# Beacon attention feeding a two-layer MLP: the first q and k loads move from the hardware queues to the software queue, and the planner's orders around them change

## The chip, the cores and the metric

The kernel runs on one core of a Trainium2 chip. The metric is the device time of one execution in microseconds (us), smaller is better. The time before is the median of 10 runs. All times below are from runs of the kernel before, or from one execution of it taken with the hardware profiler.

## The reference, cut to what matters

```
k_all = concat([beacon_k, k], axis=2)        # 16 beacons + 576 keys, per batch (8) and head (8), D = 64
v_all = concat([beacon_v, v], axis=2)
scores = (q @ k_all^T) / 8                   # causal over the 576, beacons always seen
a = exp(scores - max) / (sum + 1e-9)
x = (a @ v_all) as [8*576 tokens, 512]
h = x @ w_in                                 # 512 -> 2048
out = (h * sigmoid(1.702 h)) @ w_out         # 2048 -> 512, float32
```

Inputs are float32 in HBM; the kernel computes in float16 with float32 sums in PSUM.

## The kernel before, in words

The attention is cut into 32 *pairs*: pair i is batch i // 4 and two heads. For each pair the scores are made keys by queries, in four chunks of columns: `qk_chunk` on PE (TensorE) into one of two score tiles `s`, then `exp_chunk` on ACT into one of two tiles `E`, then the causal part is masked by `mask_chunk`, on DVE or POOL. Then the sums against `vb` follow on PE: for pairs 0 to 3 `av_both`, whose part z = 1 multiplies the ones columns of `vb` (the sums of the softmax) and whose part z = 0 multiplies the values; later pairs use `av_half`. DVE turns the sums into reciprocals and writes the normalised rows to `xT` (`norm_both`, `norm`). When 512 tokens of `xT` are there, `mlp1` (64 matmuls, L516) and its activation (`mlp1_gelu`, L528) run, and its four `mlp2` blocks (L538) are laid between the pairs that follow. The first `mlp1` needs the rows of pairs 0 to 3.

q and k must stand with D on the partitions. For batches 0 and 1 PE transposes them (`tr_pe`, L190) out of the tile `g`, and `tr_pe_out` (L198) copies the result from PSUM to `qT` and `kT`; a transpose of k or q serves one pair. For batches 2 to 7 DVE transposes squares (`tr_squares`, L253), DVE or POOL orders them (`tr_order`, L262), and SP writes them to DRAM and reads them back. Beacons of k of batches 0 and 1 come by `load_bk6` and `cast_bk6`; those of the other six by `load_bk` (8 DMAs on SP, L128) and one `cast_bk` (L136).

Two kinds of queues load. SP and ACT issue hardware-queue DMAs[...]. POOL issues the software queue, which converts float32 to float16 under way; it carries nearly all of q, k, v and the weights, in the order of POOL's instructions. POOL goes through a ring of eight semaphores: a DMA waits until the one eight places earlier has landed, and whatever stands behind it on POOL (masks, too) waits with it.

In the kernel before, q and k of the first two heads come as float32 on the hardware queues (`load_f32`: k on SP, q on ACT) into tiles `O`, and ACT and DVE cast them into `g` (`cast_f32`, L165).

The order on each engine is written by a planner in the kernel (`issue`): every piece of work is a `Work` with an engine or a choice of engines, a guessed duration, a key, needs, and "after" (not planned before that one's start). The planner only fixes the order of each engine's instructions; at run time an instruction waits for its data and its buffers, and for nothing else. Small fillers (`warm`, L1043, a matmul on zeros) are planned where PE would idle in the first 60 us. From the first `mlp1` on, the order on PE is mostly written out by `chain`.

Of the kernel before, what the change touches and what calls it, by code (L numbers as in the profile page):

```python
# [16 lines left out]
def kernel(  # L17
# [64 lines left out]
    def make_keep():  # L82
# [8 lines left out]
            channel_multiplier=-1,  # L91
        )

    w1t = cst.tile([P, NKP, DFF], F16, tag="w1", name="w1")
    w2t = cst.tile([P, NNT, DMODEL], F16, tag="w2", name="w2")
    xT = cst.tile([P, NKP, RING * S], F16, tag="xT", name="xT")
# [46 lines left out]
    def load_qk6(b, h0, h1, w):  # L143
        if b not in nat6:
            nat6[b] = gp.tile([TP, 2, H, TR * D], F16, tag="g", name="g")
        nc.gpsimd.dma_start(
            out=nat6[b][:, w, h0:h1, :],
            in_=(q, k)[w][b, h0:h1].rearrange("h (p t) d -> p h (t d)", t=TR),
        )

    def load_f32(w, eng):

        s = op_.tile([P, 2, S], F32, tag="O", name="O")
        stg[w] = s
        dict(SP=nc.sync, ACT=nc.scalar)[eng].dma_start(
            out=s.rearrange("p x s -> p (x s)")[0:TP, 0 : 2 * TR * D].rearrange(
                "p (h c) -> p h c", h=2
            ),
            in_=(q, k)[w][0, 0:2].rearrange("h (p t) d -> p h (t d)", t=TR),
        )  # L160

    def cast_f32(w, eng):
        if 0 not in nat6:
            nat6[0] = gp.tile([TP, 2, H, TR * D], F16, tag="g", name="g")
        copy[eng](  # L165
            out=nat6[0][:, w, 0:2, :].rearrange("p h c -> p (h c)"),
            in_=stg[w].rearrange("p x s -> p (x s)")[0:TP, 0 : 2 * TR * D],
        )

    def load_bk6(b):  # L170
# [148 lines left out]

    scs = {}  # L320

    def qk_chunk(i, ci):
        b, p = divmod(i, NPAIR)
        qT, kT = qTs[b % 2], kTs[b % 2]
        sc = pss.tile([P, 2, 512], F32, tag="s", name="s")
        scs[(i, ci)] = sc
        o = 0
        for (j, a, e) in CH[ci]:
            for x in range(2):
                r = 64 * x  # L330
                nc.tensor.matmul(  # L331
                    sc[:, x, o : o + e - a],
                    kT[r : r + 64, p, j * P : (j + 1) * P],
                    qT[r : r + 64, p, a:e],
                    start=True,
                    stop=True,
                )
            o += e - a

    def exp_chunk(i, ci):  # L340
# [240 lines left out]
    )  # L581
    SEM, QS = 0.1, 0.1
    SPL, CAP = 2.0, 2.0
    NBOTH = 4
    HWQ = 3

    def use(buf, *ws):
        buf.users += ws
# [2 lines left out]
    Lq, V, W1, W2 = {}, {}, [], []  # L591
    kTb, qTb, vbb, xTb = {}, {}, {}, {}
    placed = {}
    bkB = None
    pk = {}
    trp = {}
    mkeep = Work("POOL", 0.3, -4.95, make_keep)
    midn = Work("POOL", 0.6, -5.95, lambda: make_identity(nc, ident))

    bk6, stw, cst0 = {}, {}, {}  # L600
    stb = {w: Buf("O") for w in (1, 0, "bk")}
    stw[1] = Work("SP", 0.6, -9, lambda: load_f32(1, "SP"), alloc=stb[1], dma=0.7)
    stw[0] = Work("ACT", 0.6, -9, lambda: load_f32(0, "ACT"), alloc=stb[0], dma=0.7, after=[stw[1]])
    for b in range(NB2):
        ob = Buf("osb")
        x = Work("SP", 0.6, -8 + b, lambda b=b: load_bk6(b), alloc=ob, dma=0.1, after=[stw[1]])
        bk6[b] = Work(
            dict(ACT=0.6, DVE=0.6) if b else dict(ACT=0.6), 0, (-8, 1.5)[b],
            lambda eng, b=b: cast_bk6(b, eng), [x],
        )  # L610
        use(ob, bk6[b])
    g0 = Buf("g")
    for w in (1, 0):
        cst0[w] = Work(
            {("DVE", "ACT")[w]: 0.85}, 0, -8.5 - 0.1 * w, lambda eng, w=w: cast_f32(w, eng),
            [stw[w]],
        )
        use(stb[w], cst0[w])

    def first_loads(b):  # L620
        k0 = 4 * b
        kl = (-6, -4.4)[b]
        gb6 = g0 if b == 0 else Buf("g")
        lds = {(0, 1): cst0[1], (0, 0): cst0[0]} if b == 0 else {}
        got = []
        for (h0, h1) in ((2, 4), (4, H)) if b == 0 else ((0, 4), (4, H)):
            for w in (1, 0):
                x = Work(
                    "POOL", 0.7, kl + 0.1 * h0 + 0.02 * (1 - w) + (h0 == 4),
                    lambda b=b, h0=h0, h1=h1, w=w: load_qk6(b, h0, h1, w),  # L630
                    alloc=None if got else gb6, dma=0.37 * (h1 - h0), after=got[:1],
                )
                got.append(x)
                for p in range(h0 // 2, h1 // 2):
                    lds[(p, w)] = x
        if b == 0:
            for x in cst0.values():
                x.after.append(got[0])
        x = None
        for p in range(NPAIR):  # L640
            for w in (1, 0):
                if p == 1 and w == 1:
                    ub = Buf("u")
                    x = Work(
                        "PE", 0.3, k0, lambda b=b: tr_pe_beacon(b), [bk6[b], midn], alloc=ub,
                        after=[x],
                    )
                    y = Work(
                        dict(ACT=0.3, DVE=0.25), 0, k0, lambda eng, b=b: tr_pe_beacon_out(b, eng),
                        [x], after=[pk[(b, 0, 1)]],  # L650
                    )
                    use(ub, y)
                ub = Buf("u")
                kk = 4 * b + p - 0.5
                x = Work(
                    "PE", 0.55, kk, lambda b=b, p=p, w=w: tr_pe(b, p, w), [lds[(p, w)], midn],
                    alloc=ub, after=[x] if x else [],
                )
                use(gb6, x)
                trp[(b, p, w)] = x  # L660
                z = Work(
                    {("DVE", "ACT")[w]: 0.7} if b + p == 0 else dict(ACT=0.66, DVE=0.76), 0, kk,
                    lambda eng, b=b, p=p, w=w: tr_pe_out(b, p, w, eng),
                    [x], alloc=(qTb, kTb)[w][b] if p == 0 else None,
                    after=[pk[(b, 0, w)]] if p else (),
                )
                use(ub, z)
                pk[(b, p, w)] = z
        pk[b] = y
        if b == 0:  # L670
            bk6[1].after.append(pk[(0, 0, 1)])

    for b in range(B):
        kTb[b], qTb[b], vbb[b] = (Buf(f"{n}{b % 2}") for n in ("kT", "qT", "vb"))
# [4 lines left out]
        for g in range(2) if b >= NB2 else ():  # L679
            for w in (1, 0):  # L680
# [24 lines left out]
                need = []  # L705
                if w == 1:
                    if bkB is None:
                        ld4 = [
                            Work(
                                "SP", 1.2, -6 + x, lambda x=x: load_bk(x),  # L710
                                alloc=stb["bk"] if x == 0 else None, dma=0.2,
                            )
                            for x in range(HG)
                        ]
                        for x, y in zip(ld4, ld4[1:]):
                            y.after.append(x)
                        bkB = [Work(dict(ACT=0.85, DVE=0.85, POOL=0.9), 0, 3, cast_bk, ld4)]
                        use(stb["bk"], *bkB)
                    need = [Work(
                        "DVE", 0.25, k0, lambda b=b, g=g: tr_beacon(b, g),  # L720
                        bkB, after=cp[:1],
                    )]
# [45 lines left out]
    for i in range(NSTEP):  # L768
# [5 lines left out]
        for c in range(len(CH)):  # L774
            s_ = Buf("s")
            qk_ = Work(
                "PE", CHW[c] / 2400 + 0.05, i + (0, 0.01, 0.4, 0.41)[c],
                lambda i=i, c=c: qk_chunk(i, c),
                [pk[(b, p, 0)], pk[(b, p, 1)], pk[b]] if b < NB2
                else [placed[(b, hf, 0)], placed[(b, hf, 1)]],  # L780
                alloc=s_, mode=1,
            )
# [11 lines left out]
            exps.setdefault(i, []).append(ex)  # L794
            use(s_, ex)
            nm = sum(1 for (j, a, e) in CH[c] if a == s0s[j])
            mk = Work(
                dict(DVE=0.46 * nm, POOL=0.41 * nm), 0, i + 0.3,
                lambda eng, i=i, c=c: mask_chunk(i, c, eng), [ex, mkeep],
            )  # L800
            use(Eb, mk)
            for (j, a, e) in CH[c]:
                ready.setdefault(j, []).append(mk if a == s0s[j] else ex)
        vb_ = [V[(b, j)] for j in range(NJ)] + [on[b % 2]]
# [3 lines left out]
        if i < NBOTH:  # L808
            for z in (1, 0):
                for half in range(2):  # L810
# [1 line left out]
                    ub[(half, z)] = Buf("u")  # L812
                    js = sorted({j for (j, lo, hi, col) in mm})
                    av = Work(
                        "PE", sum(hi - lo for (j, lo, hi, col) in mm) / 2400 + 0.15,
                        i + 1.05 + 0.2 * (1 - z) + 0.1 * half,
                        lambda i=i, half=half, z=z: av_both(i, half, z),
                        [r for j in js for r in ready[j]] + vb_, alloc=ub[(half, z)],
                        after=avs[-1:],
                    )  # L820
                    avs.append(av)
# [65 lines left out]
        w.needs.append(exps[i][0])  # L887

    trp[(0, 1, 1)].after.append(qks[(0, 1)])
    bkB[0].after.append(exps[0][3])  # L890

# [70 lines left out]
    def issue():  # L964
# [7 lines left out]
        while todo:  # L972
            best = None
            for w in todo:
# [17 lines left out]
                        t = max([t] + [x.t1 + SEM + QS * w.mode for x in old.users])  # L992
                for a in w.after:
                    t = max(t, a.t0)
                eng = min(w.opts, key=lambda e: max(t, free[e]) + w.opts[e] + BIAS[t > 45].get(e, 0))
                t = max(t, free[eng])
                if w.dma:
                    t = max(t, landed[eng][-8] + CAP)
# [9 lines left out]
            if eng == "PE":  # L1008
                d += 0.1 * (w.mode != mode)
                mode = w.mode  # L1010
            if w.key >= 1e6 and t < 7:
                d = 0.43
            w.t0 = t
            free[eng] = t + d
# [63 lines left out]
```

The softmax here doesn't subtract the row's maximum and nothing guards it: scores larger than these inputs give would overflow.

## Time and profile before

| | |
|---|---|
| median of 10 runs | 368.17 us (367.43 to 368.67) |
| profiled execution, time | 368.0 us |
| its span, first to last instruction | 366.3 us |
| PE busy | 353.1 us, 96% of the span |
| DVE, ACT, POOL busy | 248.8, 228.2, 153.5 us |
| software queue | 49152 packets, 18.19 MB written, 49.2% of 16 engines' span |
| start of the first `mlp1` (L516) | 35.22 us |

Times inside the profile are counted from the start of the span; 1.7 us of the execution's time lie outside it. "Idle before" in brackets is the idle time of that engine just before, with what ended it. A DMA's "landing" is counted from the start of its issue.

### The profile page before, as it was taken

Reading aid. Unit: us, or ns where it says so; the run is one execution under the profiler, and the core shown is the slowest. Engines: PE = TensorE matmul, PEld = TensorE weight load, DVE = VectorE, ACT = ScalarE, POOL = GpSimd, SP = SyncE. Lnnn points to the kernel's source line nnn. Section 1 sums busy time; section 2 is a strip of 40 time slices with the busy share of each in tenths; the row PEclk is TensorE's granted clock in tenths of the full one; section 3 lists DMA queues with packets and bytes.
Section 4 is the critical chain, followed back from the end, with each engine's and each line's share of the span. In section 5 each row is a group of like instructions: output and inputs, shape, how many; then the busy total and the mean of one; then the engine's idle time right before and its main releaser. Section 6 shows DMA issues by size and latency. Waiting matters only on the chain.

```text
span 366.3 us, 6133 instructions
## 1 busy us (share of the span) xinstructions
PE 353.1 (96%) x2349; PEld 176.5 (48%) x2349; DVE 248.8 (68%) x421; ACT 228.2 (62%) x335; POOL 153.5 (42%) x264
## 2 busy tenths in 40 slices
PE   7788999999999999999999999999999999999995
PEld 3355444444444444544455864544444454444442
DVE  5556499999999986998599949972995183010021
ACT  4678787648765776676857675677658724616200
POOL 9668567593368245754376236611430010000000
PEclk9989999999999999999999999999999999999999
DMA  9999999995699645894479537921100011000012
GB/s 142 150 206 189 188 236 236 218 115 101 194 235 174 129 130 143 129 169 138 126 108 145 163 119 136 142 80 32 59 30 29 2 57 57 2 29 29 30 57 86
DMA packets 69788, 43.41 MB, mean 119 GB/s; under 512 B 42624, under 2 KB 62080, under 8 KB 69760
## 3 DMA queue, kind: packets, MB, share of 16 engines
q0 software_dynamic: 49152, 18.19, 49.2%
q1 hardware_dynamic: 20400, 24.55, 21.3%
q8 instruction: 18, 0.29, 0.3%
q10 hardware_dynamic: 208, 0.29, 0.3%
q14 instruction: 10, 0.08, 0.1%
HBM read 44.60 MB, written 16.61 MB: 167 GB/s over the span
## 4 chain that ended last, share of the span: by engine, by line
PE 83%; DMA 8%; DVE 3%; ACT 3%; issue 1%; POOL 0%; SPq 0%; DVEq 0%; ACTq 0%
PE u L516 34%; PE u L538 34%; PE u L401 9%; PE s L331 6%; DMA g<-in_k_dram 4%; ACT E L344 2%; DMA O<-in_beacon_k_dram 2%; DMA osb<-in_beacon_k_dram 1%; DVE xT L489 1%; DVE zt L470 1%; DVE osb L551 1%; DVE O L459 1%; ACT L344 0%; POOL E L367 0%; ACT bk L136 0%
## 5 line engine op out<-in xcount | busy, mean ns | idle before, releaser
L344 ACT ACTIVATE E<-s 128x1024 f16<-128x1024 f32 (+3 forms) x128 | 103.6, 865 | 49.6 <-PE s L331 47.7
L538 PE MATMUL u<-w,g 128*128 128x512 f16 x576 | 129.2, 380 | 0.6 <-DVE O L459 0.4
L516 PE MATMUL u<-xT,w 128*128 128x512 f16 (+1 forms) x640 | 126.0, 358 | 0.0
L528 ACT ACTIVATE g<-u 128x512 f16<-128x512 f32 x144 | 85.1, 597 | 42.7 <-PE u L516 42.4
L367 POOL TENSOR_SCALAR_AFFINE_SELECT E<-E 128x256 f16<-128x256 f16 (+2 forms) x148 | 64.5, 455 | 83.5 <-ACT E L344 83.3
L516 PEld LDWEIGHTS <-w 128*128 128x128 f16 x640 | 62.0, 98 | 61.4 <-issue 0.9
L538 PEld LDWEIGHTS <-g 128*128 128x128 f16 x576 | 54.5, 98 | 65.4 <-issue 3.6
L551 DVE COPY osb<-u 128x512 f32<-128x512 f32 x30 | 20.5, 683 | 65.3 <-PE u L538 65.0
L459 DVE COPY O<-u 128x240 f32<-128x240 f32 (+1 forms) x84 | 34.8, 440 | 24.7 <-PE u L401 22.4
L262 POOL COPY t<-sq 128x576 f16<-128x576 f16 x21 | 26.7, 1272 | 48.2 <-DVE sq L253 41.9
L401 PE MATMUL u<-E,vb 128*128 128x240 f16 x392 | 46.7, 266 | 0.2
L489 DVE TENSOR_TENSOR xT<-O,rz 64x576 f16<-64x576 f32 x56 | 44.3, 792 | 0.8
L470 DVE STREAM_TRANSPOSE zt<-O 64x576 f32<-64x576 f32 x56 | 43.1, 770 | 1.4
L401 PEld LDWEIGHTS <-vb 128*128 128x128 f16 x392 | 32.2, 98 | 17.2 <-issue 7.6
L331 PE MATMUL s<-qT,kT 64*128 64x80 f16 (+5 forms) x384 | 37.1, 287 | 2.9 <-ACT E L344 1.7
L253 DVE STREAM_TRANSPOSE sq<-n 128x576 f16<-128x576 f16 x48 | 34.8, 746 | 6.8 <-DMA n<-in_k_dram 6.4
L221 POOL DMA_DIRECT2D vb<-in_v_dram x40 | 34.4, 868 | 4.0 <-DMA w<-in_moe_w_in_dram 3.3
L262 DVE COPY t<-sq 128x576 f16<-128x576 f16 x27 | 26.9, 994 | 0.3
L331 PEld LDWEIGHTS <-kT 64*128 64x128 f16 x384 | 13.1, 95 | 27.1 <-issue 19.3
L480 DVE STREAM_TRANSPOSE rz<-rt 128x576 f32<-128x576 f32 x32 | 24.4, 763 | 0.6
L459 ACT COPY O<-u 128x336 f32<-128x336 f32 (+1 forms) x28 | 10.7, 429 | 2.9 <-PE u L401 2.7
L1043 PE MATMUL u<-wu 128*128 128x512 f16 x29 | 10.2, 448 | 1.3 <-DVE wu L1036 1.3
(44 smaller groups left out, 124.8 us busy)
## 6 DMA issues: line engine op xcount, KB each, us to landing
out_dram<-osb SPq DMA_DIRECT2D x36, 256.0 KB, 2.1
d<-t SPq DMA_DIRECT2D x12, 296.0 KB, 2.4
kT<-d SPq DMA_DIRECT2D x12, 296.0 KB, 3.5
n<-in_k_dram POOLq DMA_DIRECT2D x12, 288.0 KB, 5.0
n<-in_q_dram POOLq DMA_DIRECT2D x12, 288.0 KB, 6.2
d<-t SPq DMA_DIRECT2D x12, 288.0 KB, 2.4
qT<-d SPq DMA_DIRECT2D x12, 288.0 KB, 3.3
vb<-in_v_dram POOLq DMA_DIRECT2D x24, 128.0 KB, 5.6
```

Source lines behind the costliest of these rows:

```text
L253: nc.vector.transpose(sqs[(b, g, w)][:, c * n : (c + 1) * n, :, :], nat[(b, g, w)][:, c * n : (c + 1) * n, :],)
L262: copy[eng](out=tqk[(b, g, w)][:, e, o : o + S].rearrange("p (r t) -> p r t", t=TPP), in_=sqs[(b, g, w)][:, :, e, :].rearrange("p t r -> p ...
L331: nc.tensor.matmul(sc[:, x, o : o + e - a], kT[r : r + 64, p, j * P : (j + 1) * P], qT[r : r + 64, p, a:e], start=True, stop=True,)
L344: nc.scalar.activation(out=Es[i][:, :, choff[ci] : choff[ci] + w], in_=scs[(i, ci)][:, :, 0:w], func=AFT.Exp, scale=0.125,)
L367: nc.gpsimd.affine_select(out=blk, in_=blk, compare_op=ALU.is_ge, fill=0.0, base=mc, pattern=[[0, 2], [1, w]], channel_multiplier=-1,)
L401: nc.tensor.matmul(u[:, lo:hi], vb[0:kw, j, :, :].rearrange("r h c -> r (h c)")[:, o : o + 2 * D], E[0:kw, x, col : col + hi - lo], start= ...
L459: copy[eng](out=Os[i][:, x, AQ[half] : AQ[half + 1]], in_=avu[(i, x, half)][:, :])
L470: nc.vector.transpose(zst[i][0][64 * x : 64 * x + 64, :, :], Os[i][64 * (1 - x) : 64 * (1 - x) + 64, x, :])
L489: vec[eng].tensor_tensor(out=xT[r : r + 64, p, c : c + S], in0=Os[i][r : r + 64, x, :], in1=zst[i][2][r : r + 64, :], op=ALU.mult,)
L516: nc.tensor.matmul(u[:, o : o + w], w1t[:, kp, nt * P : (nt + 1) * P], xT[:, kp, m : m + w], start=(kp == 0), stop=(kp == NKP - 1),)
L528: nc.scalar.activation(out=gts[g][:, nt, :], in_=hu[(g, nt)][:, :], func=AFT.Gelu_apprx_sigmoid)
L538: nc.tensor.matmul(o[:, :], gts[g][:, nt, mt * P : (mt + 1) * P], w2t[:, nt, :], start=(nt == 0), stop=(nt == NNT - 1),)
```

## The change

- `load_f32`, `cast_f32` and the two casts are gone. q and k of heads 0 and 1 are now the first two DMAs of POOL's software queue, ahead of the making of `ident`; heads 2 and 3 follow behind `ident`, then `keep`, then the values of batch 0, then heads 4 and 5, and 6 and 7, in pieces of two heads where four were loaded at once.
- `load_bk` is planned after the first exp of pair 2 (`BKE = 2`), and `cast_bk` may go to any engine. On SP the order is now: the two `load_bk6`, then the eight DMAs of `load_bk`, then the rest.
- The part z = 1 of `av_both` no longer lists the values' loads among its needs; its guessed duration and some keys change. A tile `neg` is made by one DVE instruction; the masking on PE that would use it is switched off (`NMASK = 0`), so `pe_mask` is false everywhere and all masks stay as they are.
- The planner therefore gives other orders. On ACT the cast of the beacons (`cast_bk`) is gone from between the exps of pairs 0 and 1; it stands on POOL behind the mask of pair 4's first chunk. On PE the sums z = 1 of pair 0 stand ahead of the last two score chunks of pair 1, the values' part behind them. Before the exps of pair 2 ACT copies kT and qT of pair 2 and kT of pair 3; between those of pairs 2 and 3 it copies qT of pair 3 and kT, qT of pair 4; between those of pairs 3 and 4, kT of pair 5. `mlp1` now stands behind all of chunks 0 and 1 of pair 5 on PE, and the transposes of pairs 6 and 7 all stand behind `mlp1` (before, that of pair 6's k stood ahead of it and only chunk 0 of pair 5). On POOL the blocks j = 1 and j = 2 of batch 1's values are issued one behind the other, and all four masks of pair 3 that POOL makes (chunks 1 to 3) stand right behind them; before, the block j = 3 stood between the masks of chunk 1 and those of chunks 2 and 3.

From the second half of pair 4's sums on, the order on PE is the same in both.

```
-    mkeep = Work("POOL", 0.3, -4.95, make_keep)
-    midn = Work("POOL", 0.6, -5.95, lambda: make_identity(nc, ident))
-    stw[1] = Work("SP", 0.6, -9, lambda: load_f32(1, "SP"), alloc=stb[1], dma=0.7)
-    stw[0] = Work("ACT", 0.6, -9, lambda: load_f32(0, "ACT"), alloc=stb[0], dma=0.7, after=[stw[1]])
+    mkeep = Work("POOL", 0.3, -5.6, make_keep)
+    mneg = Work("DVE", 0.2, -5, make_neg, [mkeep])
+    midn = Work("POOL", 0.6, -5.97, lambda: make_identity(nc, ident))
...
-        for (h0, h1) in ((2, 4), (4, H)) if b == 0 else ((0, 4), (4, H)):
+        for (h0, h1) in ((0, 2), (2, 4), (4, 6), (6, H)) if b == 0 else ((0, 4), (4, H)):
             for w in (1, 0):
                 x = Work(
-                    "POOL", 0.7, kl + 0.1 * h0 + 0.02 * (1 - w) + (h0 == 4),
+                    "POOL", 0.7, kl + 0.1 * h0 + 0.02 * (1 - w) + (b == 0) * (h0 >= 4) + (b == 1) * (h0 == 4),
...
-                        "PE", sum(hi - lo for (j, lo, hi, col) in mm) / 2400 + 0.15,
+                        "PE", sum(hi - lo for (j, lo, hi, col) in mm) / 2400 + 0.06,
-                        [r for j in js for r in ready[j]] + vb_, alloc=ub[(half, z)],
+                        [r for j in js for r in ready[j]] + (vb_[-1:] if z else vb_), alloc=ub[(half, z)],
...
+                        sbk = Buf("O")
+                        bkl4 += [
...
-    bkB[0].after.append(exps[0][3])
+    bkl[1].after.append(exps[0][2])
+    bkl4[0].after.append(exps[BKE][0])
...
-            if w.key >= 1e6 and t < 7:
+            if w.key >= 1e6 and t < 5:
```

## The prediction

> **What bounds the kernel now.** I read the page first, then the chain that ended last, then the timelines of ACT and POOL over the first 36 us, then a table by windows. Page: PE is full from the third slice on; the DMA engines are full for the first nine slices (82 us).
>
> ```profile
> PE   7788999999999999999999999999999999999995
> DMA  9999999995699645894479537921100011000012
> ```
>
> So after about 65 us the time is PE's own work, and what a start-up change can win is an earlier first `mlp1`, handed on undiminished. The chain of waits, first 66 us:
>
> ```profile
> 6.50 8.09 DMA O<-in_beacon_k_dram
> ...
> 14.81 0.83 ACT bk L136
> ...
> 18.35 15.48 DMA g<-in_k_dram
> ...
> 33.87 0.45 PE u L190 x12
> 34.32 0.65 PE u L1043 x2
> 34.96 0.32 PE s L331 x2
> 35.28 13.93 PE u L516 x64
> 49.24 0.60 ACT g L528
> 49.85 1.28 ACT L344
> 51.15 3.14 ACT E L344 x4
> ```
>
> Two loads are on it: the beacons, for which ACT stops, and pair 6's k, which the transposes ahead of L516 wait for. But a chain shows one releaser per step; ACT's timeline shows what follows the beacon stall:
>
> ```profile
> 8.54 3.42 ACT L344 ACTIVATE E<-s 128x1024 f16<-128x1024 f32 x4 [1.16 <-PE s L331]
> 14.81 0.83 ACT L136 CAST bk<-O 128x768 f16<-128x768 f32 x1 [2.85 <-DMA O<-in_beacon_k_dram]
> 15.55 3.12 ACT L344 ACTIVATE E<-s 128x1024 f16<-128x1024 f32 x4
> ...
> 20.94 1.91 ACT L344 ACTIVATE E<-s 128x1024 f16<-128x1024 f32 x2
> 24.54 1.35 ACT L344 ACTIVATE E<-s 128x928 f16<-128x928 f32 x2 [1.69 <-PE s L331]
> ...
> 33.42 1.35 ACT L344 ACTIVATE E<-s 128x928 f16<-128x928 f32 x2 [0.43 <-PE s L331]
> ```
>
> These are the exps of pairs 0, 1, 2 and 4. Pair 2's begin at 20.94, not behind pair 1's (18.67), because heads 4 to 7 land late: PE stands until 19.13 for "DMA g<-in_q_dram". A second gate is on POOL:
>
> ```profile
> 28.11 0.89 POOL L221 DMA_DIRECT2D vb<-in_v_dram  x1 [0.97 <-DMA w<-in_moe_w_in_dram]
> 29.00 1.02 POOL L367 TENSOR_SCALAR_AFFINE_SELECT E<-E 128x224 f16<-128x224 f16 x3
> 30.16 0.88 POOL L221 DMA_DIRECT2D vb<-in_v_dram  x1
> 31.04 0.78 POOL L367 TENSOR_SCALAR_AFFINE_SELECT E<-E 128x256 f16<-128x256 f16 x2
> ```
>
> POOL waits until 28.11 for the second piece of w1 (the ring of eight), issues a block of values, and pair 3's masks come behind; two of them behind yet another block, done at 31.82. Pair 3's sums end at about 33.0, and the exps of 33.42 follow them.
>
> **The change part by part.**
>
> *First loads.* Before, k and q were in `g` at 5.84 and 6.45 (casts at 5.01 and 5.67, 0.83 and 0.78 long). Now k's issue moves to 0.81 and q's to 1.55 on POOL. Nearest rows: the first two software loads of before, the same shape, issued at 1.55 and 2.29, landed after 5.3 and 6.0 us. That gives 6.1 and 7.5, so q is 1.1 late. [...] Here the row decides, its 5.3 and 6.0 holding the queueing that is there. [...] I take +0.8. Exps of pair 0: 8.54 + 0.8 = 9.3. Moved on POOL: `ident` by the two issues (1.4) to about 2.8, needed at 6; heads 2 and 3 to about 2.8 and 3.5, landing 8.1 and 9.5, just as the transposes come; values from 3.45 to 5.5.
>
> *Beacons and their cast.* ACT's stall goes: 2.85 + 0.83. But "loaded later" does not hold on the chip: `after` places the eight DMAs in SP's order, SP has nothing to wait for ahead of them, and they will start at about 1.7, not later than 2.21. So the DMA engines win nothing from it; what is won is the cast's place. On POOL it costs 0.8 to 1.3 (L136 took 0.83 on ACT; POOL's 576-column copy took 1.27) behind pair 4's first mask, ahead of nothing before `mlp1`. Exps of pair 1 then end at 9.3 + 3.42 + 3.12 + 0.62 (the second beacon cast, moved in) = 16.5 instead of 18.67.
>
> *What is late next: heads 4 to 6.* The software queue carries 295 KB more ahead of pair 3's data, the hardware queues 590 KB less. Rates: 375 GB/s from 3.0 to 3.75 us, when the float32 loads ran; about 205 written (so 410 read) when the converting queue ran alone:
>
> ```profile
> 16.00:17.00 1.00, 0.60 (x4) 0.30 (x5) 0.90 (x3) 1.00 (x2) 0.77 (x3) 1.00 1.33 212
> ```
>
> 590 / 375 = 1.6 us taken off, 295 / 205 = 1.4 us put on: about even. So heads 4 to 7 land at the same byte count as before, the last at 19.05, but in four pieces of 0.72 us: q of 4 and 5 at 17.6, k of 6 and 7 at 18.3. PE transposes that k by 18.8; ACT's copies of pair 2 (2 x 0.65) are done by 18.6, that of pair 3's k at 19.5. Exps of pair 2: 19.5, against 20.94.
>
> *Copies moved to ACT.* Between there and the first gelu ACT now makes four copies of 0.65 (2.6) where it made 0.65 + 0.22 + 0.67 + 0.65 (2.2), and the last of those no longer stands before pair 4's last exp. If the 26 remaining matmuls of pair 1's sums run at full clock (1.5 us), pair 3's exps start at 19.5 + 1.9 + 0.4 (PE's lag) + 1.35 + 3 x 0.65 = 25.1 and pair 4's at 25.1 + 1.9 + 1.35 + 0.65 + 0.35 = 29.4.
>
> *The clock.* Before, PE idled over 18 to 19 and then ran at half clock:
>
> ```profile
> 18.00:19.00 1.00, 0.12 (x6) 0.00 (x0) 0.00 (x0) 1.00 (x3) 1.00 (x3) 1.00 1.32 203
> ...
> 22.00:23.00 1.00, 1.00 (x16) 0.81 (x14) 0.40 (x1) 0.85 (x1) 0.67 (x1) 0.50 1.26 210
> ```
>
> At that clock those sums take 2.5 us and everything on ACT is 1.0 later (pair 4's exps at 30.4). [...] I take full; half stays in the range.
>
> *The gate on POOL* has the same bytes ahead: w1's second piece again at 28.05. Then 0.9 issue and four masks of 0.35 with nothing between: done at 30.4 instead of 31.8. Pair 3's sums: two thirds done, 26 matmuls from 30.6, end 32.05 (before 33.0). Score chunk and lag 0.4: pair 4's chunk 2 exp at 32.45 (33.42), chunk 3 ends 33.8; pair 5's second score chunk needs that buffer, 0.35; filler 0.25: L516 at 34.4, against 35.22. With the half clock ACT sets it instead: pair 4's second exp ends at 32.4, the last at 33.8 to 34.3, L516 at 34.9. That the k of pair 6 (33.83) and its transposes (0.45) leave the path is in this.
>
> *Nothing-cost edits.* `neg` (one DVE instruction near 4.5, like the 0.18 memset; DVE next acts at 7.6); more masks of pairs 0 and 1 on DVE (0.28 each, DVE is half idle before 35); fillers. Uncovered, 0.1 to 0.5.
>
> **Behind L516.** Its 13.93, the last gelu 0.60 and the table load 1.28 are unchanged, so ACT moves along. DVE is the doubt: it was gapless from 41.35 to 54, after a 6.42 wait for "DMA n<-in_k_dram", and that landing stays. The new order puts the copies of pair 4's sums three operations earlier on DVE, where it waits for L516's end. From there I add up DVE's list to the release of the third `mlp2` with the gaps between starts seen before (copies 0.3 and 0.42, transposes 0.7 to 0.8, `norm` 0.8, `tr_order` 1.0): 22.1, which gives L516's end + 22.5; before it was 71.62 - 49.17 = 22.45. So the gain passes on whole, less 0.05.
>
> **Sum:** 368.0 (the profiled execution, 0.17 below the median) - 0.82 + 0.05 = 367.2; as a median 367.4.
>
> **The rivals.**
>
> *Slower: the software queue pays in full for the 295 KB.* If the hardware loads had run in room that the software queue cannot use (it starts 1.7 us after them: first packets in 3.75 to 4.5 against 1.5 to 2.25), everything behind lands 295 / 205 = 1.4 later: w1's second piece at 29.5, L516 at 35.8, 0.6 late; with the half clock as well 1.1. It decides when heads 6 and 7's k lands after 19.7. For it: the values are issued 2 us later. Against: the full DMA row. 369.0.
>
> *The cover moves, no gain:* the half clock and a little of that: L516 at 34.9 to 35.2, or DVE's wait for pair 4's sums costs what was won. 368.0.
>
> *More is won:* if written bytes limit the engines, 295 KB are saved: 1.4 us at 205, the gates come to 17 and 26.7, L516 at 33.2 to 33.5. The gain is capped at 1.4 there: w2's last piece landed at 60.32 (POOL waited for it), and the first `mlp2`, started at 59.10, needs it from its 13th matmul, at about 61.7. Against: 375 written in the float32 stage. 366.6.
>
> **How the numbers follow.** Forecast 0.50 (366.9 to 367.9), no gain 0.13, more won 0.16, slower 0.21. A measurement of this kernel can tell about 0.2% (0.74 us) from no change; the forecast straddles that on the fast side: of its 0.50, 0.32 faster. Faster 0.32 + 0.16 = 0.48; slower 0.21; within 0.31. Range 366.1 to 369.1, from beyond the middle of "more won" to that of "slower".
>
> **What would show it.** Right: no ACT wait for beacons; SP's eight beacon loads before 8 us; exps of pair 2 near 19.5; w1's second piece near 28; L516 near 34.4; clock 1.0 over 20 to 24. Wrong: heads 6 and 7's k after 19.7; half clock at 20 to 24; DVE waits at the second or third `mlp2`.

## The result, and the profile after

The changed kernel is slower: median 372.02 us (370.26 to 374.53, 9 runs) against 368.00 us of the kernel before on the same chip; ratio 1.0112, 95% interval 1.0097 to 1.0127. The profiled execution took 371.81 us, with a span of 370.1 us: 3.8 more than before. The helpers' lines have moved: `mlp1` is L520, `mlp2` L542 and its copy out of PSUM (`osb`) L555, `av_half` L405, `av_out` L463, `norm` L493, DVE's mask L364, POOL's L371, `tr_order` L249, the exps L348.

The start-up went better than forecast. The slices of the page (PE, DMA), then rows of ACT's timeline: the exps of pairs 0, 2, 3 and the last two of pair 4.

```profile
PE   7999986999998999999999999999999999999995
DMA  9999999995479935795379647931100011000012
```

```profile
8.16 1.89 ACT L348 ACTIVATE E<-s 128x1024 f16<-128x1024 f32 x2 [0.88 <-PE s L322]
...
20.20 3.14 ACT L348 ACTIVATE E<-s 128x1024 f16<-128x1024 f32 x4
...
24.81 3.19 ACT L348 ACTIVATE E<-s 128x1024 f16<-128x1024 f32 x4
...
30.95 1.35 ACT L348 ACTIVATE E<-s 128x928 f16<-128x928 f32 x2 [0.63 <-PE s L322]
```

Between the exps ACT waits for no beacons any more (0.69 us, at 2.77, is left ahead of them), and POOL issues its gated block of values at 26.65 instead of 28.11:

```profile
26.65 0.88 POOL L208 DMA_DIRECT2D vb<-in_v_dram  x1 [1.62 <-DVE rt L480]
27.53 1.40 POOL L371 TENSOR_SCALAR_AFFINE_SELECT E<-E 128x256 f16<-128x256 f16 x4
```

The profile names a DVE instruction as the releaser there, but it had ended at 26.37; in a1 and a3, which start alike, others are named. And 28.11 was late for the kernel before: in b1 and c3, which start as it does, the block is issued at 27.26 and 27.59. So about half of the lead belongs to the execution.

`mlp1` starts at 32.89 instead of 35.22 (its first 15 matmuls, in a view that ends at 36 us), and the first `mlp2` 2.5 us ahead:

```profile
32.89 3.40 PE L520 MATMUL u<-xT,w 128*128 128x512 f16 x15
```

Then PE's timeline loses it, and more:

```profile
56.60 3.63 PE L542 MATMUL u<-w,g 128*128 128x512 f16 x16
...
61.64 0.32 PE L405 MATMUL u<-E,vb 128*128 128x240 f16 x2 [0.20 <-DVE O L463]
64.74 0.72 PE L405 MATMUL u<-E,vb 128*128 128x336 f16 x5 [2.78 <-DVE osb L555]
...
65.92 5.31 PE L542 MATMUL u<-w,g 128*128 128x512 f16 x16
...
73.61 3.63 PE L542 MATMUL u<-w,g 128*128 128x512 f16 x16
...
84.95 0.71 PE L405 MATMUL u<-E,vb 128*128 128x336 f16 x5 [0.32 <-DVE osb L555]
...
112.57 0.71 PE L405 MATMUL u<-E,vb 128*128 128x336 f16 x5 [1.23 <-DVE osb L555]
```

Before, PE had no wait of over 0.3 us at this place:

```profile
63.05 1.86 PE L401 MATMUL u<-E,vb 128*128 128x240 f16 x14
64.84 0.60 PE L331 MATMUL s<-qT,kT 64*128 64x512 f16 x8
65.59 3.61 PE L538 MATMUL u<-w,g 128*128 128x512 f16 x16
```

The five sums at 64.74 need a `u` buffer, and the one that comes free holds the first `mlp2`, which DVE copies out only at 63.99. Behind the wait PE's clock was half: 16 matmuls in 5.31 us instead of 3.63. The table by windows (PEclk is the number before the last two) dates it:

```profile
66.00:68.00 2.00, 2.00 (x5) 0.64 (x6) 1.96 (x4) 1.76 (x2) 1.03 (x2) 0.50 0.98 340
68.00:70.00 2.00, 2.00 (x8) 0.80 (x7) 1.94 (x4) 0.00 (x0) 1.51 (x4) 0.66 0.66 107
```

Start against start of the same work, after minus before: first `mlp2` -2.50, second +0.33, third +1.99, second `mlp1` +2.50 (86.13 against 83.63), the third `mlp2` behind it +3.88 (113.75 against 109.87), and so to the end.

So DVE is late. Its groups from 41 to the third `osb` copy behind the second `mlp1` (before: to 113.6; after: to 117.5); norms and masks, before and then after; the columns are busy us, mean ns, idle:

```profile
L489 DVE TENSOR_TENSOR xT<-O,rz 64x576 f16<-64x576 f32 x14 | 10.9, 781 | 0.2
L360 DVE TENSOR_TENSOR E<-E,keep 128x256 f16<-128x256 f16 (+2 forms) x8 | 1.8, 260 | 0.3 <-ACT E L344 0.3
```

```profile
L493 DVE TENSOR_TENSOR xT<-O,rz 64x576 f16<-64x576 f32 x14 | 14.0, 1000 | 0.2
L364 DVE TENSOR_TENSOR E<-E,keep 128x256 f16<-128x256 f16 (+1 forms) x8 | 2.8, 391 | 0.1
```

As many instructions, 4.1 us more. The single rows tell which (first those of before, two norms and the first `osb` copy), and POOL's timeline of the same stretch tells beside what:

```profile
57.95 1.61 DVE L489 TENSOR_TENSOR xT<-O,rz 64x576 f16<-64x576 f32 x2
...
63.46 0.68 DVE L551 COPY osb<-u 128x512 f32<-128x512 f32 x1
```

```profile
56.83 1.49 DVE L493 TENSOR_TENSOR xT<-O,rz 64x576 f16<-64x576 f32 x1
58.34 2.05 DVE L493 TENSOR_TENSOR xT<-O,rz 64x576 f16<-64x576 f32 x1
61.62 1.18 DVE L364 TENSOR_TENSOR E<-E,keep 128x256 f16<-128x256 f16 x1
63.99 0.69 DVE L555 COPY osb<-u 128x512 f32<-128x512 f32 x1
```

```profile
57.64 1.71 POOL L249 COPY t<-sq 128x576 f16<-128x576 f16 x1
59.87 0.76 POOL L371 TENSOR_SCALAR_AFFINE_SELECT E<-E 128x224 f16<-128x224 f16 x1
61.13 1.17 POOL L249 COPY t<-sq 128x576 f16<-128x576 f16 x1
```

A norm takes 0.75 us undisturbed, a mask of this size 0.29. The second norm stands 1.01 us beside the POOL copy (until 59.35), the mask 0.68 us beside the next one (until 62.30): 0.75 + 1.01 = 1.76 of 2.05, and 0.29 + 0.68 = 0.97 of 1.18. The first norm seems to have waited for the last of four masks that POOL made in a row (until 57.70: 0.87 + 0.75 = 1.62, measured 1.49). POOL pays too, where DVE was there first: 1.71 for a copy that takes 1.17, 0.76 for a mask that takes 0.39. That looks like taking turns, a wait for neither data nor buffers. DVE's transposes of squares beside such copies (POOL's at 42.27 and 44.83, 1.18 and 1.19) keep their time: 0.78 at 42.14, 0.73 at 44.70.

These POOL copies are halves of `tr_order` for batch 2's last q. In the kernel before one of them was made by POOL at 50.47, beside squares and PSUM copies, the other by DVE (0.70 us at 54.52). The new plan puts the copies of pair 4's sums ahead of those squares, so the squares come at 54.4 and 55.25, and both halves go to POOL. A third such copy, of batch 3's first k, meets the norms at 80.27 (2.89 us for two).

### The profile page after: what moved, and what is told of

The parts are those of the page before. It is cut to its first block, busy times and chain, and to the rows that moved or that the text cites. A ratio compares the mean times of both kernels' runs of the same rounds, so it can differ in the third digit from the quotient of the medians.

```text
span 370.1 us, 6145 instructions
## 1 busy us (share of the span) xinstructions
PE 355.2 (96%) x2351; PEld 176.4 (48%) x2351; DVE 250.4 (68%) x427; ACT 228.9 (62%) x336; POOL 154.9 (42%) x260
## 4 chain that ended last, share of the span: by engine, by line
PE 67%; DVE 3%; ACT 1%; DMA 1%; issue 1%; SPq 0%
PE u L542 28%; PE u L520 26%; PE u L405 7%; PE s L322 5%; ACT E L348 1%; DMA qT<-d 1%; DVE osb L555 1%; DVE xT L493 1%; DVE t L249 1%; DVE sq L240 0%; DVE O L463 0%; DVE rz L484 0%; DVE zt L474 0%; SPq L259 0%; DVE rt L480 0%
## 5 line engine op out<-in xcount | busy, mean ns | idle before, releaser
L348 ACT ACTIVATE E<-s 128x1024 f16<-128x1024 f32 (+3 forms) x128 | 103.8, 869 | 47.7 <-PE s L322 46.1
L542 PE MATMUL u<-w,g 128*128 128x512 f16 x576 | 130.9, 383 | 0.4 <-DVE O L463 0.4
L520 PE MATMUL u<-xT,w 128*128 128x512 f16 (+1 forms) x640 | 126.0, 358 | 0.0
L371 POOL TENSOR_SCALAR_AFFINE_SELECT E<-E 128x256 f16<-128x256 f16 (+2 forms) x138 | 61.1, 460 | 86.8 <-ACT E L348 86.7
L520 PEld LDWEIGHTS <-w 128*128 128x128 f16 x640 | 62.1, 98 | 61.3 <-issue 0.7
L542 PEld LDWEIGHTS <-g 128*128 128x128 f16 x576 | 54.8, 98 | 66.5 <-issue 5.8
L555 DVE COPY osb<-u 128x512 f32<-128x512 f32 x29 | 19.9, 685 | 66.1 <-PE u L542 66.0
L463 DVE COPY O<-u 128x240 f32<-128x240 f32 (+1 forms) x83 | 34.4, 435 | 25.6 <-PE u L405 23.2
L405 PE MATMUL u<-E,vb 128*128 128x240 f16 x392 | 47.0, 266 | 4.6 <-DVE osb L555 4.3
L249 POOL COPY t<-sq 128x576 f16<-128x576 f16 x22 | 28.4, 1290 | 50.8 <-DVE sq L240 44.0
L493 DVE TENSOR_TENSOR xT<-O,rz 64x576 f16<-64x576 f32 x56 | 47.5, 849 | 0.8
L405 PEld LDWEIGHTS <-vb 128*128 128x128 f16 x392 | 32.3, 97 | 21.9 <-issue 11.7
L249 DVE COPY t<-sq 128x576 f16<-128x576 f16 x26 | 26.0, 1000 | 0.3
L463 ACT COPY O<-u 128x336 f32<-128x336 f32 (+1 forms) x29 | 11.5, 432 | 7.5 <-PE u L405 7.4
L1040 PE MATMUL u<-wu 128*128 128x512 f16 x31 | 12.1, 488 | 1.3 <-DVE wu L1033 1.3
```

The costliest lines, as they stand in the source:

```text
L249: copy[eng](out=tqk[(b, g, w)][:, e, o : o + S].rearrange("p (r t) -> p r t", t=TPP), in_=sqs[(b, g, w)][:, :, e, :].rearrange("p t r -> p ...
L348: nc.scalar.activation(out=Es[i][:, :, choff[ci] : choff[ci] + w], in_=scs[(i, ci)][:, :, 0:w], func=AFT.Exp, scale=0.125,)
L371: nc.gpsimd.affine_select(out=blk, in_=blk, compare_op=ALU.is_ge, fill=0.0, base=mc, pattern=[[0, 2], [1, w]], channel_multiplier=-1,)
L405: nc.tensor.matmul(u[:, lo:hi], vb[0:kw, j, :, :].rearrange("r h c -> r (h c)")[:, o : o + 2 * D], E[0:kw, x, col : col + hi - lo], start= ...
L463: copy[eng](out=Os[i][:, x, AQ[half] : AQ[half + 1]], in_=avu[(i, x, half)][:, :])
L493: vec[eng].tensor_tensor(out=xT[r : r + 64, p, c : c + S], in0=Os[i][r : r + 64, x, :], in1=zst[i][2][r : r + 64, :], op=ALU.mult,)
```

## The experiments

Theory A: POOL's copies beside DVE's two-input instructions, in a stretch where DVE sets the time. Its rivals are in the expectations. Each edit is made behind the planner, on its finished order (`work(...)` picks one piece, `move(x, y)` puts x before y), so that nothing else is planned anew. "Before" in the ratios is the kernel before, run beside.

**a1: the two late copies on ACT.**

```
+    for e in range(2):
+        work("tr_order", 2, 1, 0, e).eng = "ACT"
```

> The changed kernel, but the two ordering copies of batch 2's last q (128x576 f16), which POOL made at 57.64 and 61.13 us beside DVE's norm and mask instructions, are made by ACT. Theory A (POOL's f16 copies slow DVE's two-operand instructions down, and DVE is the engine that sets the time from 55 to 117 us): the two norms of pair 4 go back from 1.5 and 2.05 to 0.75 us each and the two masks of pair 7 from 0.77 each to 0.2 to 0.3, the copy of the first mlp2 is made near 61.2 instead of 63.99, PE does not wait 2.78 us, the second mlp2 keeps the full clock: 367.5 to 369.5. Theory B (DVE's instructions are long by themselves, and the loss is only that the first mlp2's copy stands behind masks and transposes in DVE's order): norms stay at 1.5 to 2 us, time within 0.7 of 372.0. Theory C (the loss is the half clock after PE's wait, whatever causes the wait): the time follows the wait alone, 370 if it stays above 1 us.

368.48 us, ratio 1.0007 (0.9993 to 1.0022): of the 4.0 us of loss 0.3 are left. DVE's rows:

```profile
58.35 0.79 DVE L493 TENSOR_TENSOR xT<-O,rz 64x576 f16<-64x576 f32 x1
59.16 0.87 DVE L493 TENSOR_TENSOR xT<-O,rz 64x576 f16<-64x576 f32 x1
...
61.25 0.29 DVE L364 TENSOR_TENSOR E<-E,keep 128x256 f16<-128x256 f16 x1
...
62.53 0.69 DVE L555 COPY osb<-u 128x512 f32<-128x512 f32 x1
```

The longest PE wait at that place is 0.19 us and the second `mlp2` runs at full clock. The `osb` copy was 1.3 us later than expected, because this execution's `mlp1` began at 34.38. Theory A holds, B falls. One point is open: POOL's four masks stood beside the norms here too, but now the norms kept their time and the masks were stretched (2.47 us for the four, 1.41 in the changed kernel). Why the norm at 56.83 there waited for masks, and this one did not, no run tells.

**a2: the first `osb` copy on ACT, the collisions left.**

```
+    work("mlp2_out", 0, 0).eng = "ACT"
```

> The changed kernel, but the PSUM copy of the first mlp2 is made by ACT, which is idle then, instead of DVE at 63.99 us. Nothing else is moved. PE's wait of 2.78 us and the half clock of the second mlp2 should go under every theory. Theory A (DVE is short of time through the collisions with POOL): DVE is relieved by one copy of 0.69 us and by the 1.1 us that it idled for the slow mlp2, but the norms stay at 1.5 to 2 us each, so DVE is late again before 117 us: 369.8 to 370.8. Theory B (only the place of that copy) and theory C (only wait and clock): the 4.5 us of wait and clock come back whole: 367.3 to 368.3.

370.34 us, ratio 1.0050 (1.0034 to 1.0066), inside A's interval. The two norms still take 3.65 us, and the wait comes back a little further on, for the next PSUM copy in DVE's list, this time with the clock kept:

```profile
64.82 3.61 PE L542 MATMUL u<-w,g 128*128 128x512 f16 x16 [1.84 <-DVE O L463]
```

So wait and half clock at 65 us are not the whole loss: at full clock 2.2 of the 4.0 us remain, which C did not expect.

**a3: DVE's and POOL's order of before for batch 2's squares.**

```
+    first = work("av_out", 4, 0, 0)
+    for w in (
+        work("tr_squares", 2, 1, 1, 1), work("tr_order", 2, 1, 1, 0), work("tr_order", 2, 1, 1, 1), work("tr_beacon", 2, 1),
+        work("tr_squares", 2, 1, 0, 0), work("tr_squares", 2, 1, 0, 1), work("tr_order", 2, 1, 0, 0),
+    ):
+        move(w, first)
+    work("tr_order", 2, 1, 0, 1).eng = "DVE"
+    move(work("tr_order", 2, 1, 0, 1), work("av_out", 4, 1, 1))
```

> The changed kernel, but DVE and POOL do batch 2's squares and ordering copies in the order of the kernel before, ahead of the copies of pair 4's sums; the last ordering copy is on DVE again. The masks and norms that follow are not beside a POOL copy. Theory A: norms of pair 4 about 0.75 to 0.8 us, masks of pair 7 0.2 to 0.3, the first mlp2's copy at 61 to 62, no long PE wait: 367.0 to 369.0. Theory B (place of the copy in DVE's list, which is kept here): 371 to 372.5. PE may wait up to 1.5 us more for pair 4's copies, near 48 us, where it had fillers.

368.58 us, ratio 1.0019 (1.0006 to 1.0032). Norms of pair 4 together 1.81 us, no PE wait at 64 us. As A had it.

**a4: `mlp1` 2.2 us later.**

```
         hu[(g, nt)] = u
+        for x in range(10) if g + nt == 0 else ():
+            nc.tensor.matmul(u[:, :], wu[:, 0:P], wu[:, :], start=True, stop=True)
```

> The changed kernel with ten matmuls on zeros (128x512, 0.216 us each) ahead of the first mlp1, so that mlp1 starts 2.2 us later, about where it stood in the kernel before. Its result is not touched. Theory D (PE runs ahead of DVE, whose time is set by when batch 2's first load lands and by its own list; being early is what costs): nothing is lost by the delay, the wait shrinks below 1 us and the half clock goes: 369.5 to 371. Theory A: DVE's list waits for pair 4's sums at 47 us and so is moved along, the collisions with POOL stay: 373 to 374.3.

374.97 us, ratio 1.0189 (1.0161 to 1.0217): almost 3 us more than the changed kernel, even above A's interval. The norms take 3.58 us again and PE waits 2.47 us. Being early was not the harm (D falls).

**b1: one useless POOL copy in the kernel before,** beside pair 4's norms.

```
+        nc.gpsimd.tensor_copy(
+            out=dum.rearrange("p (r t) -> p r t", t=16), in_=wu.rearrange("p (t r) -> p r t", r=32)
+        )
...
+    order.insert(order.index(work("load_qk", 3, 0, 1)), d)
```

> The kernel before with one added POOL instruction that nobody needs: an f16 copy of zeros (128x512, in the strided order of the ordering copies, to a tile of its own) just ahead of the load of batch 3's first k, that is from about 57.9 us, beside the two norms of pair 4 (57.95 to 59.57 us there). Theory A (a POOL copy slows DVE's two-operand instructions): the two norms together take 2.7 to 3.5 us instead of 1.61, DVE is later by that, and since DVE sets the time there: 369.0 to 370.0 against 368.2. Theory B (no such slowing): norms stay at 1.6, POOL's masks come up to 1.2 us later where they have room: 368.0 to 368.6.

368.59 us, ratio 1.0013 (1.0006 to 1.0020): slower, by less than expected. The time would fit the rival too (368.0 to 368.6); what speaks for A is that the norms are longer, 2.25 us for two instead of 1.61, and that PE waits 0.74 us for the `osb` copy behind them. DVE's norms and POOL's copy:

```profile
57.84 0.73 DVE L489 TENSOR_TENSOR xT<-O,rz 64x576 f16<-64x576 f32 x1
58.59 1.51 DVE L489 TENSOR_TENSOR xT<-O,rz 64x576 f16<-64x576 f32 x1
```

```profile
57.83 1.65 POOL L1044 COPY dum<-wu 128x512 f16<-128x512 f16 x1
```

The first norm ran through and the copy was stretched; the second waited for the rest of the copy (until 59.48: 0.75 + 0.89 = 1.64, measured 1.51). So the copy cost DVE about what was left of it when DVE's instruction came up, 0.64 us here, not its whole length per norm.

**b2 and b3: the two halves of the change alone.** b2 is the changed kernel with the needs and duration of `av_both` put back; b3 is the kernel before with

```
-                        "PE", sum(hi - lo for (j, lo, hi, col) in mm) / 2400 + 0.15,
+                        "PE", sum(hi - lo for (j, lo, hi, col) in mm) / 2400 + 0.06,
-                        [r for j in js for r in ready[j]] + vb_, alloc=ub[(half, z)],
+                        [r for j in js for r in ready[j]] + (vb_[-1:] if z else vb_), alloc=ub[(half, z)],
```

> The half of the change that concerns loads and beacons, with the planner's needs and guessed durations of av_both as in the kernel before. The planner's order then has batch 2's last ordering copy split: half on POOL in front of pair 7's masks, about beside pair 4's norms, half on DVE. Theory A: the start is 1 to 2.5 us earlier, one POOL copy collides and costs DVE 1 to 1.5: 367.8 to 370.0, and the norms of pair 4 are long (over 2 us for the two). If the changed start itself were what costs (rival: the software queue's later data), the time is 371.5 or more with short norms.

368.34 us, ratio 0.9999 (0.9985 to 1.0013). The time is as expected; the norms were short (1.61 for two), since the POOL copy came at 60.39 beside DVE's own ordering copy. In the median the loads alone cost nothing, and they bring nothing.

> The other half alone: the kernel before, where only the needs of the sums z = 1 and the guessed duration of av_both are changed. The planner then puts one of batch 2's ordering copies on POOL behind batch 2's values, a little ahead of pair 4's norms. Theory A: the start is as before, pair 4's norms or pair 6's masks are stretched if the copy falls beside them: 368.2 to 369.8. Rival (the needs alone bring the change's loss): 371 or more.

372.27 us, ratio 1.0104 (1.0084 to 1.0124): a miss. The needs of z = 1 on the values' loads and a guess of 0.09 us, which change no instruction's work, cost 4.1 us, as much as the whole change. Which of the two does it was not tested. The norms of pair 4 were short (1.61), but DVE came to the first `osb` copy at 65.32 (before: 63.46), by other entries: a third transposed copy, an ordering copy and a mask stretched.

```profile
54.08 0.75 DVE L198 COPY qT<-u 128x576 f16<-128x576 f16 x1
55.96 1.45 DVE L262 COPY t<-sq 128x576 f16<-128x576 f16 x1
58.24 0.82 DVE L360 TENSOR_TENSOR E<-E,keep 128x224 f16<-128x224 f16 x1
65.32 0.68 DVE L551 COPY osb<-u 128x512 f32<-128x512 f32 x1
```

PE waits 2.21 us for it, and 1.27 us at 91 us, behind norms of 2.64 us beside a POOL copy.

**d1: b3 with the shares and the order of before from 41 to 58 us alone.**

```
+    first = work("av_out", 4, 0, 0)
+    for w in (
+        work("tr_beacon", 2, 1), work("tr_squares", 2, 1, 0, 0), work("tr_squares", 2, 1, 0, 1), work("tr_order", 2, 1, 0, 0),
+    ):
+        move(w, first)
+    work("tr_order", 2, 1, 0, 0).eng = "POOL"
+    work("tr_order", 2, 1, 0, 1).eng = "DVE"
+    move(work("tr_order", 2, 1, 0, 1), work("av_out", 4, 1, 1))
+    work("tr_pe_out", 1, 3, 0).eng = "ACT"
```

> The needs half alone (b3: 372.27 us), but in the stretch from 41 to 58 us DVE, POOL and ACT share and order batch 2's squares, ordering copies and the copies of pair 7's transposed q as in the kernel before. Everything after 58 us stays in b3's order. Theory A' (b3's early loss is DVE's list ahead of the first mlp2's copy: a third transposed copy of 0.75 us, an ordering copy of 1.45 and a mask of 0.82 us): DVE reaches that copy near 63.4 instead of 65.32, PE's wait of 2.21 us shrinks below 0.5, no half clock; what lies behind (norms of 2.64 us beside a POOL copy at 87.8, PE's wait of 1.27 at 91) may stay: 368.2 to 370.0. Rival (b3's loss comes from after 58 us, or from PE's order): 371.3 or more.

368.85 us, ratio 1.0021 (1.0013 to 1.0030): 3.4 of 4.1 us come back, and the wait of 1.25 at 87 us is still there. So in that half, too, the early loss is DVE's list.

**c2 and c3: the first seven `osb` copies on ACT,** in b3 and in the kernel before.

```
+    for g, n in ((0, 0), (0, 1), (0, 2), (0, 3), (1, 0), (1, 1), (1, 2)):
+        work("mlp2_out", g, n).eng = "ACT"
```

> The needs half alone (b3, 372.27 us, which was 2 us more than theory A had put), but with the PSUM copies of the first seven mlp2 blocks on ACT. Theory A': also there the loss is DVE's lateness in front of the first mlp2's copy (its list has a third copy of the transposed q or k, 0.75 us, and slowed copies and masks, 1.3 us), so with 4.8 us taken off DVE the waits of 2.21 and 1.27 us go: 367.5 to 369.0. Rival (the loss is on PE, in the interrupted second mlp1 at 89 us, or on ACT): 370.5 or more.

371.74 us, ratio 1.0100 (1.0064 to 1.0137): a miss. The four runs lie in two pairs, near 370.2 and 373.3, and the profile is of one of the fast pair. The buffer that PE waits for is now one that DVE copies behind two norms (2.93 us, "DVE O L459", at 66.56). Relieving DVE behind the crowded place does not help.

> The kernel before, with nothing but the PSUM copies of the first seven mlp2 blocks on ACT. It tells what relief of DVE is worth without the change's start. Theory A: PE waits for DVE there only 0.3 and 0.41 us, so 367.3 to 368.0; if c1 is faster than this one by over 0.7 us, the changed start is worth that once DVE keeps up. Rival (the relief of DVE alone explains c1 and b4): the same time as c1.

368.94 us, ratio 1.0021 (1.0012 to 1.0030): slower, where a gain was expected. PE waits 0.70 us for DVE at 64.85 and 0.44 us for ACT's own `osb` copy at 83.67.

**c1, d2, b4, c4: towards a better kernel.** d2 lets DVE make the three colliding copies; c1 is d2 with the seven `osb` copies on ACT; b4 is a3 with them; c4 is c1 with batch 2's first loads issued ahead of a block of values.

```
+    for e in range(2):
+        work("tr_order", 2, 1, 0, e).eng = "DVE"
+    work("tr_order", 3, 0, 1, 0).eng = "DVE"
...
+    for x in ((2, 0, 1), (2, 0, 0)):
+        move(work("load_qk", *x), work("load_v", 1, 3))
```

The last two lines are c4's alone.

> The changed kernel with the three POOL copies that fell beside norms (both of batch 2's last q, one of batch 3's first k) made by DVE itself, and the PSUM copies of the first seven mlp2 blocks on ACT. Nothing else is moved. Theory A: DVE gains 7 x 0.69 = 4.8 us for the moved PSUM copies and 3.1 + 1.2 us of collisions, and pays 3 x 0.65 = 2 us for the copies; so it is early at every place where PE waited for it in the changed kernel (64.7, 85, 112.6, 120.2 us), and PE stands 1.5 to 2 us ahead of the kernel before to the end: 365.8 to 367.2. If the start's gain is lost in other ways (rival: DMA or ACT), 367.5 to 369.

366.65 us, ratio 0.9964 (0.9951 to 0.9977): faster than both kernels.

> As c1 (the three POOL copies that fell beside norms are made by DVE), but the PSUM copies of the mlp2 blocks stay on DVE. It separates c1's two edits: c2 and c3 showed that the moved PSUM copies bring nothing or cost 0.8 us. Theory A (the collisions are the loss): 366.3 to 367.8, at most 1 us above c1. Rival (c1's gain was DVE's relief by the PSUM copies): 369 or more, since DVE gets 2 us of copies more.

369.37 us, ratio 1.0041 (1.0018 to 1.0065): a miss, the rival's value. The norms are at 0.76, but the copies cost DVE 1.21 + 0.65 + 0.83 us and it is still late. PE's wait at the same place, in d2 and in c1:

```profile
64.17 0.71 PE L405 MATMUL u<-E,vb 128*128 128x336 f16 x5 [1.74 <-DVE osb L555]
```

```profile
64.20 3.61 PE L542 MATMUL u<-w,g 128*128 128x512 f16 x16 [0.79 <-DVE O L463]
```

Without the collisions and without the `osb` copies DVE nearly keeps up: PE's wait there shrinks from 1.74 to 0.79 us. The first edit is not enough by itself (d2). The second was not run alone on the changed kernel; it gained nothing on the kernel before (c3) and next to nothing on b3 (c2).

> The changed kernel with DVE's and POOL's order of the kernel before for batch 2's squares (as in a3), and the PSUM copies of the first seven mlp2 blocks on ACT instead of DVE. Theory A with its second half (DVE is the engine that sets the time from 55 to 117 us, which is why a1 and a3 gave no more than the kernel before): 4.8 us are taken off DVE, PE's waits of 0.34, 1.27 and 0.41 us for DVE go: 366.0 to 367.3, faster than both kernels. Rival (ACT has no room, or PE alone sets the time): 368.0 to 369.5.

367.49 us, ratio 0.9987 (0.9977 to 0.9997): faster, just above the interval; the norms at 76 us still met a POOL copy (2.01 us for one).

> As c1, and the loads of batch 2's first k and q are issued on POOL ahead of block j = 3 of batch 1's values. DVE should begin its squares 2 to 3 us earlier (about 38 instead of 40.8 us). Theory A with DVE as the bound from 40 us on: 0 to 0.7 us less than c1. If DVE is no longer the bound in c1: the same as c1 within 0.5; if the values come too late for pair 4's sums at 46.7 us or POOL's masks are held up: up to 1 us more.

366.92 us, ratio 0.9972 (0.9960 to 0.9983): the same as c1 within the intervals. DVE began its squares at 38.41 instead of 40.72, and that brought nothing: its start is no longer what limits there.

## Why the prediction was wrong

- *Start-up: right in kind, too cautious.* Forecast: first exp 9.3, pair 2's exps 19.5, values' block 28.05, `mlp1` 34.4. Measured: 8.16, 20.20, 26.65, 32.89. q came no later (+0.8 was taken, the author's estimate; it was issued at 2.12 and transposed at 6.40, 4.3 us behind, where 6.0 was taken). The clock, which the prediction took as full by estimate alone, was full from 14.76 to `mlp1`; it was half from 7.93 to 14.76. That was luck in part: in a1 and a3, whose order up to `mlp1` is the same, the half clock came at 29.99 to 33.41 and 30.24 to 33.65 (a filler took 0.61 us there, 0.39 behind it), and `mlp1` began at 34.38 and 34.34; in a2 it came at 8.26 to 15.09, and `mlp1` began at 32.71. So the start gave a lead of 0.9 to 2.5 us, and 34.4 came true only with a half clock just ahead of `mlp1`, for which the prediction had 34.9. The block at 26.65 and `mlp1` at 32.89 are at or ahead of the figures of "more is won" (26.7; 33.2 to 33.5), but since the start varies so much they do not show its reason, that written bytes limit.
- *"From there I add up DVE's list ... 22.1, which gives L516's end + 22.5 ... So the gain passes on whole, less 0.05": this is the step that failed.* Measured, the third `mlp2` starts 26.7 us behind `mlp1`'s end (73.61 - 46.87), 4.2 more. The terms: two norms at 0.8 each were 3.55 together (+1.95), and two masks of pair 7 1.54 instead of 0.45 (+1.1); these 3 us are PE's wait of 2.78. The second `mlp2` took 5.31 instead of 3.6 at half clock (+1.7), which the sum did not have at all. Wait and clock make 4.5; 0.3 of it was made good elsewhere. I took durations from a trace in which no POOL copy stood beside a norm and added up DVE's list alone; that POOL's list put `tr_order` beside it was in the new order, and was left out.
- *What bounds the kernel: half read.* "PE is full from the third slice on" misreads the row, which has 8 in the third and fourth slice and 9 from the fifth (37 us). And "the time is PE's own work" left out DVE, whose row of the same page is full from the sixth to the fourteenth slice (46 to 128 us):

```profile
DVE  5556499999999986998599949972995183010021
```

  The chain of waits of before, of which the prediction shows the part up to the exps of 51.15, runs on through DVE from there to the second `mlp2`:

```profile
60.37 0.41 DVE O L459
...
63.46 0.68 DVE osb L551
64.17 0.92 DVE xT L489
65.12 0.42 DVE O L459
...
65.59 0.59 PE u L538 x2
```

  So DVE had no time to spare there even before, and what was added to its list could reach PE at once.
- *The places named as what would prove it wrong* were right: PE waits for DVE ahead of the second `mlp2`, and DVE then 1.11 us for that `mlp2`, before its copy at 71.27.
- *The rivals.* "Slower" had the sign with another cause, heads 4 to 7 late; pair 2's exps began 0.74 us earlier than before, so that cause did not occur. "No gain" allowed for DVE only what was won.
- *Nothing-cost edits.* The needs of z = 1 and its guessed duration were treated as a part of the start. They alone bring a loss of the same size (b3), the loads do not (b2): the planner turns needs and a guess of 0.09 us into another sharing of work among DVE, POOL and ACT up to 40 us later. But b3 loses its time at other entries of DVE's list than the changed kernel does, so that the two losses are alike in size is not explained.

Shown: the collisions (b1 made one, a1 took two away), DVE's list as the limit (a1, a3, d1, c1), and that the needs half alone loses as much, the loads half nothing (b2, b3). Read from durations only: the half clock's price of 1.7 us; no run had the changed kernel's wait with a full clock. Open: why the first norm waited for masks; 0.3 us of the norm at 58.34 beyond the copy's end, and b3's ordering copy of 1.45 us, which stood beside POOL's DMA issues alone, where another of 0.69 (at 52.31 of the changed kernel) was not stretched. b3's loss behind 58 us was not taken apart.

## What to carry to other kernels

When a plan is made anew, add up each engine's new list with durations that hold beside the neighbour it will have: in b1 DVE's norm beside a POOL copy cost 0.64 us on top, about what was left of that copy. Look for the engine that has almost no gaps (DVE from 41 to 117 us here), not only for the busiest; an earlier start is handed on only if that engine also gets its work done earlier. And test an edit of a planner's guesses by itself, even if it changes no instruction.

## What the hardware did that I had not expected

- DVE's norm and POOL's copy took turns: the norm's 0.75 us became 2.05, and the copy's 1.17 became 1.71; the 0.39 of POOL's mask became 0.76.
- An ordering copy f16 to f16 (128x576, SBUF to SBUF) took 1.21 and 1.20 us on ACT (a1), though ACT's copies of that size out of PSUM take about 0.65; on DVE alone it takes about 0.65 (a3, at 53.76), and 1.17 or 1.18 beside POOL's (at 45.36 after, at 48.41 before).
- The half clock came in one piece of 3.41 us, from 65.96 to 69.37. In the traces of both kernels the clock changed a whole number of such pieces apart: before, half from 7.38 to 10.80 (1) and from 21.04 to 24.45 (1), with 10.24 us of full clock between (3); after, half from 7.93 to 14.76 (2), then full for 51.20 us to 65.96 (15, of 3.413 us each). The length of the wait did not decide by itself: the changed kernel waited 2.78 us and the clock fell after, c2 waited 2.93 us and it was kept. In this stage it went with how busy PE had been in the piece before. For c2 and a2 the place of the pieces is an estimate, counted on from the end of an earlier half clock of the same trace: in c2 from 24.02, 12 pieces before 64.98, in a2 from 15.09, 14 pieces before 62.87. PE's busy time is the first column behind the length; the changed kernel and c2:

```profile
62.55:65.96 3.41, 1.22 (x14) 0.68 (x14) 3.35 (x8) 0.47 (x2) 0.51 (x2) 1.00 1.34 212
```

```profile
64.98:68.39 3.41, 1.83 (x16) 0.93 (x16) 2.98 (x6) 0.70 (x1) 0.48 (x1) 1.00 1.09 252
```

  In c2 the wait was split between two such pieces (2.06 us of work in the one from 61.57). After 1.08 (a4), 1.22 and 1.33 us (b3) of work the clock was halved (the second `mlp2` took 5.24, 5.31 and 4.19 us), after 1.57 (a2) and 1.83 it was kept (3.61 and 3.63). This holds for these five runs in this stage of large matmuls, and what decides was not shown: in the kernel before the clock fell at 21.04 behind 3.41 us with 2.05 us of mostly small transposes, more work than kept it in a2.
